# PSUM banks by turns, denser weight splits and a reordered first root in an attention and gated feed-forward kernel

## The chip, the cores and the metric

The kernel runs on one core of one Trainium2 chip. A core has a matrix engine (PE, TensorE) with its own weight loads, and VectorE (DVE), ScalarE (ACT), GpSimd (POOL) and SyncE (SP); here SP only issues DMAs. PE writes to PSUM, which has eight banks; DVE and ACT read PSUM, POOL does not. Each engine works through its own list of instructions in order, and semaphores hold it where it needs another engine's result. The metric is the time of one execution on the device in microseconds (us).

## The reference

All tensors are float32. Attention has 8 batches, 8 heads, 576 positions and heads of 64; the first four heads see the last 32 positions, the other four every fourth of the last 128. Its output, 4608 rows of 512, goes through a normalization by the root of the mean square and a gated feed-forward layer of width 1536:

```python
scores = where(mask[h], q @ k.T / sqrt(64), -1e9)        # per batch and head
attn = exp(scores - max) / (sum + 1e-9)
x = (attn @ v) -> rows of 512
xn = x / sqrt(mean(x * x) + 1e-6) * rms_g
g, val = xn @ w_gate, xn @ w_val                         # 512 -> 1536
out = (g * sigmoid(g) * val) @ w_out                     # 1536 -> 512
```

## The kernel before, in words

**Items.** The 4608 rows are worked in 16 items `u` of 288 rows, each half of one batch. An item has two kinds of work: its attention, in 14 bursts (a pair of heads `c` and a block `i` of rows), and its feed-forward, in 12 slices `j` of 128 of the 1536 columns. While item u's feed-forward runs, the attention of item u+1 is woven into it.

**Steps.** The main loop (L783 to L811) has a step `t` for every third of a slice: part 0 is the gate (L643: 128 columns of `w_gate` by the four chunks of xn, which accumulate in one PSUM bank), part 1 the value (L667, same form with `w_val`), part 2 the projection (L693) of the slice before, which adds into four banks acc0 to acc3. Item u has the steps 36u to 36u+35. Ahead of the main loop run 25 rounds `n` (L765) with the attention of item 0 alone and the first of item 1; in them `busy` (L731) puts filler matmuls on PE, whose result nobody reads, and `start` (L628) already runs gate and value of slice 0 on the unnormalized rows. Round n has the clock `now` = n; step t has now = t + 23.

**Order.** It is written out by hand. `later(dt, rank, fn)` (L110) puts work off by dt rounds or steps; `flush` (L113) issues what is due, by rank, at the start of each. So the queue of each engine is filled by step and then by rank: a normalization of scores for item 2 and later has rank -1, a product 0, the copy out of a transposition 0.2, the copy of an attention output 0.5, the tanh of a gate 0, silu 0.8, exponentials 2, weight decoding 5 and up, weight splits 6.

**A burst** goes through scores on PE (L486, or L489 from item 2 on), maximum and mask (L361, L366, DVE), exponential (L376, ACT), normalization (L384 to L391; on POOL, DVE or ACT), transposition on PE (L463) into a PSUM bank, copy to SBUF (L446 on ACT, and L448 on DVE for the low part from item 2 on), output on PE (L472, L477, L478) and copy into the rows `xraw` (L408, L411, L421). `plan` (L740) says in which round or step each of these three PE parts runs. From item 3 on, bursts come every two steps, so that their transpositions fall on all three parts in turn; those of item 1 fall on parts 0 and 1.

**The root.** When the last burst of an item is out, `square` (L423) squares each chunk of its rows, the squares are added (L433), PE sums them over the columns (L529, tile `rps`), DVE and POOL form the power -1/2 (L536, L537), DVE (and ACT, from item 1 on) spreads it into diagonal tiles (L551 and L555, or L561 for item 0), PE spreads that over the partitions (L571, tile `bps`), and DVE multiplies the rows with it (L582 for item 0, L585 later).

**Banks.** Gates always take the bank g, values the bank v, and each uses 288 of the bank's 512 columns. A transposition in the main loop writes to columns 288 to 479 of such a bank:

```python
if part == 0:   free = gate(u, j)        # the gate just written
elif part == 1: free = val(u, j)         # L805 then puts it back to this slice's gate
else:           free = v_free            # this slice's value
```

Readers of the gate's bank are tanh (ACT, L656) and silu (DVE, L661), the reader of the value's is the product (DVE, L674); a write to a bank waits for its readers. In the rounds, transpositions alternate between g and v (L772), scores between s, acc0 and acc1, outputs between o and acc2.

**Weights.** They arrive as 64-bit floats in 18 pieces of two slices; `rebase` (L151, ACT or POOL), and `shift`, `low`, `sign` or `rest`, `whole` (L164 to L183, DVE) make float32 of them during the rounds and item 0, whose matmuls use that float32 (L619). From item 1 on each weight is a sum of two rounded parts, and each gate has three matmuls (L622 to L624) for every one; `split_weight` (L227) makes the parts, high on ACT (L242), low on DVE or POOL (L243), into SBUF that earlier tiles leave free. The tuple SPLITS says at which steps: at even steps from 8 to 30, then from step 37 in four of five, until all 36 slices are done.

Of the kernel before, what the change touches and what calls it, by code (L numbers as in the profile page):

```python
# [9 lines left out]
F32 = mybir.dt.float32  # L10
# [24 lines left out]

LAG, OUT, LATER = 4, 2, 1
STEPS = (0,) * 6 + (1, 0) * 2 + (1,) * 4 + (0,) * 9 + (2, 1)
REBASES = 5, 9, 17, 20
BUSY = 7, 3
SIGNS = 4  # L40
SPLITS = 8, 31, 37


ORDER = [(0, 0, "q"), (0, 1, "q"), (0, 0, "v"), (0, 2, "q"), (0, 0, "w"), (0, 1, "v"), (0, 3, "qv"), (0, 2, "v"),
# [23 lines left out]
def attn_moe(ctx: ExitStack, tc: tile.TileContext, qk_in, v_in, w_gate, w_val, w_out, rms_g, outT):  # L68
# [41 lines left out]
    def later(dt, rank, fn):  # L110
        put_off.setdefault(now[0] + dt, []).append((rank, fn))
# [283 lines left out]
    def take(u, c, i, o):  # L395

        blocks, nq, _ = geometry(u, c)
        if (u, c) not in xraw:
            xraw[u, c] = sb.tile([P, U], F32, tag="xraw", name=f"xraw_{u}_{c}", bufs=NC)
        x = xraw[u, c]  # L400
        if c < NC // 2:
            to = x[:, QB * i:QB * i + nq]
        else:
            to = x.rearrange("p (j r) -> p r j", r=DIL)[:, i, :]
        copy = V.tensor_copy if i % 2 and u != 1 else A.copy
        if u < NNAT:
            for a in range(2):
                copy(out=to[a * D:(a + 1) * D], in_=o[a * D:(a + 1) * D, a * nq:(a + 1) * nq])  # L408
        else:
            for a in range(2):  # L410
                A.copy(out=to[a * D:(a + 1) * D], in_=o[a * D:(a + 1) * D, (2 + a) * nq:(3 + a) * nq])  # L411
        if i == len(blocks) - 1:
            later(1, 2.5, lambda: square(u, c))

    def add(u, c, i, o):
        _, nq, _ = geometry(u, c)
# [211 lines left out]
    def start(kind, c):  # L628
# [2 lines left out]
            first[kind] = ps.tile([P, 512], F32, tag={"g": "acc1", "v": "acc3"}[kind], name=f"{kind}_0_0")  # L631
        three(first[kind][:, :U], weight(kind, 0, 0), c, xraw[0, c], c == 0, c == NC - 1)

    def group(kind, u, j):

        if u + j == 0:
            return first.pop(kind)
        out = ps.tile([P, 512], F32, tag=kind, name=f"{kind}_{u}_{j}")
        for c in range(NC):
            three(out[:, :U], weight(kind, u, j), c, xs[u][c], c == 0, c == NC - 1)  # L640
        return out
# [89 lines left out]
    def busy(n):  # L731

        for _ in range(n):
            PE.matmul(busy_ps, ones, ones[:, None, :].to_broadcast([P, 4, P]), start=True, stop=True)
# [5 lines left out]
    def plan(u, base, q_at, t_at, o_at):  # L740
        for b, *ts in zip(bursts(u), q_at, t_at, o_at):
            for kind, t in zip("qto", ts):
                events.setdefault(base + t, {})[kind] = b
        events.setdefault(base + o_at[-1] + 3, {})["sum"] = u
        events.setdefault(base + o_at[-1] + (4, 7, 5)[min(u, 2)], {})["apply"] = u

    def attend(t_ps, **tags):
        e = events.pop(now[0], {})
        if any(k in e for k in "qto"):
            products(e.get("q"), e.get("t"), e.get("o"), t_ps, **tags)  # L750
        if "sum" in e:
            rms_sum(e["sum"])
        if "apply" in e:
            rms_apply(e["apply"])
# [10 lines left out]
    for n in range(ends):  # L765
        decode(STEPS[n])
        if n in REBASES:
            later(0, 8, ahead)
        flush()
        t_ps = None  # L770
        if "t" in events.get(n, {}):
            t_ps = ps.tile([P, 512], F32, tag="gv"[n % 2], name=f"t_first_{n}")[:, :2 * QB]  # L772
        attend(t_ps, s_tag=("s", "acc0", "acc1")[n % (3 if n < nb else 2)], o_tag=("o", "acc2")[n % 2])
        if n < nb + LAG + OUT:
            busy(BUSY[1])
        for kind, c in FIRST.get(n, ()):
            start(kind, c)
        if n == ends - 1:
            _, v_free = gate(0, 0), val(0, 0)
        now[0] += 1  # L780

    prev = None
    for u in range(NU):  # L783
        for j in range(NJ):
            for part in range(0 if u + j else 2, 3):
                t = 3 * (u * NJ + j) + part
                if used and (t % 5 != 1 if t >= SPLITS[2] else t % 2 == 0 and SPLITS[0] <= t < SPLITS[1]):
                    later(0, 6, lambda: split_weight(*used.pop(0), V if t < SPLITS[1] or t % 2 else G))
                if u == 0:
                    decode(1)  # L790
                opening = len(ops) <= 2
                flush()
                if opening and not late:
                    early.close()
                    late.append(ctx.enter_context(tc.tile_pool(name="late", bufs=2)))
                if part == 0:
                    free = gate(u, j)
                elif part == 1:
                    free = val(u, j)
                else:  # L800
                    if prev is not None:
                        proj(*prev)
                    prev = (u, j)
                    free = v_free
                if part == 1:  # L805
                    g_free, v_free = g_free, free
                    free = g_free
                elif part == 0:
                    g_free = free
                attend(free, s_tag="acc2" if t < 4 else "s")  # L810
                now[0] += 1  # L811
    flush()
# [69 lines left out]
```

## Time and profile before

| what | us |
|---|---|
| median of 3 runs | 1155.4 (1155.17 to 1156.75) |
| profiled execution | 1156.42 |
| its span, first to last instruction | 1154.6 |
| PE busy | 1122.5 (97%) |
| DVE busy | 790.7 (68%) |
| ACT busy | 719.3 (62%) |
| POOL busy | 618.0 (54%) |
| mean granted clock of PE | 0.999 of full |

How to read what follows: a row of a timeline is start, duration, engine, line, operation, what it writes and reads with its shape, and how many instructions are merged in it; in brackets stands the idle time of the engine just before and what ended it. Rows of the chain of waits are start, duration and what the chain ran through. A matmul's duration overlaps with the next one's, so the distance of the starts counts. A wait is put down to the semaphore that came last, which may name an instruction just beside the true one.

### The profile page before, as it was taken

To read this page: it belongs to the slowest core of one execution; us is meant where nothing else is said; L and a number is where in the kernel's file an instruction comes from. 1 tells how busy PE (TensorE), PEld (TensorE's weight loads), DVE (VectorE), ACT (ScalarE), POOL (GpSimd) and SP (SyncE) were. 2 spreads that over 40 slices of the span, in tenths; PEclk is the share of its full clock that TensorE was granted. 3 is DMA by queue.
4 is the path that set the end of the run, shared out by engine and by line. 5 is a ranking of instruction groups with operands and counts; after the bars stand their busy time and mean duration, and the time that the engine had idled before them with its cause. 6 is when DMAs were issued, how large, how long until landed. Compare 5 with 4: busy or idle time off the path is not lost.

```text
span 1154.6 us, 25970 instructions
## 1 busy us (share of the span) xinstructions
PE 1122.5 (97%) x8363; PEld 1086.7 (94%) x8363; DVE 790.7 (68%) x2900; ACT 719.3 (62%) x2602; POOL 618.0 (54%) x1074
## 2 busy tenths in 40 slices
PE   8898879999999999999999999999999999999998
PEld 6686778999999999999999999999999999999998
DVE  7889866866757586675758667585866757586421
ACT  5686576665757576575756657576765757676311
POOL 7235567655646465564646655465655646565211
PEclk9999999999999999999999999999999999999999
DMA  8556211211312122131212213131221313120000
GB/s 245 152 202 211 92 50 38 82 58 41 93 37 82 40 70 63 44 97 28 84 41 79 60 40 92 29 93 38 72 63 34 101 30 88 38 81 15 1 22 21
DMA packets 61545, 82.19 MB, mean 71 GB/s; under 512 B 7298, under 2 KB 41090, under 8 KB 61410
## 3 DMA queue, kind: packets, MB, share of 16 engines
q1 hardware_dynamic: 61410, 80.54, 23.3%
q8 instruction: 67, 1.10, 0.4%
q14 instruction: 68, 0.56, 0.2%
HBM read 71.08 MB, written 9.44 MB: 70 GB/s over the span
## 4 chain that ended last, share of the span: by engine, by line
PE 77%; DVE 15%; ACT 4%; issue 2%; POOL 1%; DMA 0%; POOLq 0%; SPq 0%; DVEq 0%; ACTq 0%
PE acc L622 8%; PE acc L623 7%; PE acc L624 7%; PE g L622 7%; PE v L622 7%; PE v L623 7%; PE v L624 7%; PE g L624 7%; PE g L623 7%; DVE qs L344 3%; PE s L489 3%; PE o L477 3%; PE g L463 2%; DVE xraw L585 2%; DVE t L366 2%
## 5 line engine op out<-in xcount | busy, mean ns | idle before, releaser
L686 POOL TENSOR_TENSOR hlo<-th,hhi 128x288 fp32r<-128x288 f32 x180 | 145.1, 806 | 193.4 <-ACT hhi L685 189.6
L624 PE MATMUL acc<-hhi,lo 128*128 128x288 f32 x720 | 212.5, 295 | 0.0
L391 POOL TENSOR_SCALAR t<-t,sum 72x72 f32<-72x72 f32 (+3 forms) x414 | 151.0, 377 | 82.0 <-DVE sum L386 72.8
L624 PE MATMUL v<-xhi,lo 128*128 128x288 f32 x612 | 180.7, 295 | 0.0
L624 PE MATMUL g<-xhi,lo 128*128 128x288 f32 x612 | 180.6, 295 | 0.0
L685 ACT CAST hhi<-th 128x288 fp32r<-128x288 f32 x180 | 78.1, 434 | 162.6 <-DVE th L674 159.3
L376 ACT ACTIVATE t<-t,sum 96x128 f32<-96x128 f32 (+3 forms) x448 | 165.7, 376 | 14.1 <-DVE sum L366 13.4
L305 POOL TENSOR_TENSOR vlo<-vt,vhi 128x128 fp32r<-128x128 f32 x196 | 94.3, 481 | 116.3 <-ACT vhi L301 99.5
L421 DVE TENSOR_TENSOR xraw<-o,xraw 64x96 f32<-64x96 f32 (+1 forms) x392 | 106.8, 272 | 60.8 <-ACT xraw L411 55.8
L656 ACT ACTIVATE th<-g 128x288 f32<-128x288 f32 x180 | 73.9, 411 | 119.1 <-PE g L624 92.3
L624 PEld LDWEIGHTS acc<-hhi,lo 128*128 128x128 f32 x720 | 135.7, 188 | 0.0
L661 DVE SCALAR_TENSOR_TENSOR th<-th,g 128x288 f32<-128x288 f32 x180 | 80.4, 447 | 68.6 <-ACT th L656 68.6
L361 DVE TENSOR_TENSOR t<-s,mask 96x256 f32<-96x256 f32 (+3 forms) x196 | 71.7, 366 | 77.8 <-PE s L489 57.2
L624 PEld LDWEIGHTS v<-xhi,lo 128*128 128x128 f32 x612 | 115.2, 188 | 0.0
L624 PEld LDWEIGHTS g<-xhi,lo 128*128 128x128 f32 x612 | 115.0, 188 | 0.0
L411 ACT COPY xraw<-o 64x96 f32<-64x96 f32 (+1 forms) x392 | 101.7, 259 | 16.3 <-PE o L478 14.0
L622 PE MATMUL g<-xhi,hi_g 128*128 128x288 f32 x357 | 110.6, 310 | 0.4 <-DVE pt L448 0.3
L622 PE MATMUL acc<-hhi,hi_o 128*128 128x288 f32 x360 | 110.9, 308 | 0.0
L335 POOL TENSOR_TENSOR ks<-qk,ks 128x288 fp32r<-128x288 f32 (+2 forms) x112 | 110.3, 999 | 0.0
L623 PE MATMUL acc<-hlo,hi_o 128*128 128x288 f32 x360 | 107.1, 298 | 0.0
L674 DVE TENSOR_TENSOR th<-th,v 128x288 f32<-128x288 f32 x180 | 81.4, 452 | 36.2 <-PE v L624 33.4
L623 PE MATMUL g<-xlo,hi_g 128*128 128x288 f32 x322 | 94.8, 294 | 0.0
(179 smaller groups left out, 3575.8 us busy)
## 6 DMA issues: line engine op xcount, KB each, us to landing
qk<-in_qk_dram SPq DMA_DIRECT2D x60, 288.0 KB, 2.8
vt<-in_v_dram SPq DMA_DIRECT2D x196, 64.0 KB, 1.9
qk<-in_qk_dram SPq DMA_DIRECT2D x30, 352.0 KB, 3.0
out_dram<-ot SPq DMA_DIRECT2D x64, 144.0 KB, 1.9
qk<-in_qk_dram SPq DMA_DIRECT2D x30, 304.0 KB, 2.8
raw<-in_w_gate_dram SPq DMA_DIRECT2D x12, 512.0 KB, 4.3
raw<-in_w_val_dram SPq DMA_DIRECT2D x12, 512.0 KB, 4.9
raw<-in_w_out_dram SPq DMA_DIRECT2D x12, 512.0 KB, 4.1
```

What stands on the lines that cost most here:

```text
L305: G.tensor_tensor(out=vl, in0=vs.pop(b), in1=vh, op=ALU.subtract)
L335: ek.tensor_tensor(out=ks[:, 1, :nkt], in0=kr, in1=ks[:, 0, :nkt], op=ALU.subtract)
L376: A.activation(out=t[:nq, a, :n], in_=t[:nq, a, :n], func=AF.Exp, scale=-1.0, bias=sm[:nq, a, 0:1], accum_out=sm[:nq, a, 1:2] if u else None)
L391: (V if u == 0 and (c, i) > (NC - 1, 0) else G).tensor_scalar(out=t[:nq, a, :n], in0=t[:nq, a, :n], scalar1=sm[:nq, a, 3:4], scalar2=1.0, ...
L411: A.copy(out=to[a * D:(a + 1) * D], in_=o[a * D:(a + 1) * D, (2 + a) * nq:(3 + a) * nq])
L421: V.tensor_tensor(out=to[rows], in0=o[rows, a * nq:(a + 1) * nq], in1=to[rows], op=ALU.add)
L622: PE.matmul(out, wh[:, cc, :], xh, start=start, stop=False)
L623: PE.matmul(out, wh[:, cc, :], xl, start=False, stop=False)
L624: PE.matmul(out, wl[:, cc, :], xh, start=False, stop=stop)
L661: V.scalar_tensor_tensor(out=t, in0=t, scalar=1.0, in1=g, op0=ALU.add, op1=ALU.mult)
L674: V.tensor_tensor(out=t, in0=t, in1=v_ps[:, :U], op=ALU.mult)
L686: G.tensor_tensor(out=lo, in0=t, in1=hi, op=ALU.subtract)
```

## The change

- Banks: gate j now takes g for even j and v for odd j, value j the other one; so gate j+1 is written to the bank of value j, and value j+1 to the bank of gate j. A transposition in part 0 goes to the gate just written (as before), in part 1 to the value just written, in part 2 to a new tile in the bank of this slice's gate.
- Splits: the first stretch begins at step 4, not 8 (even steps up to 30); from step 37 on every step has one.
- Opening: the last rebase on ACT moves from round 20 to 23; the square of item 0 gets rank 1.9 instead of 2.5; from round 17 on one filler matmul a round instead of three; in item 0 the odd bursts of the first three chunks are copied by ACT instead of DVE; the transposition of round 24 goes to acc0, the scores of rounds 21 to 24 alternate between s and acc2 instead of s and acc0.
- Item 1's sums (L529) run one step later; its root's spread (L571) stays where it was.

```diff
-REBASES = 5, 9, 17, 20
+REBASES = 5, 9, 17, 23
-SPLITS = 8, 31, 37
+SPLITS = 4, 31, 37
...
-        copy = V.tensor_copy if i % 2 and u != 1 else A.copy
+        copy = V.tensor_copy if i % 2 and u == 0 and c == NC - 1 else A.copy
...
-            later(1, 2.5, lambda: square(u, c))
+            later(1, 2.5 if u else 1.9, lambda: square(u, c))
...
+    def bank(kind, j):
+        return "gv"[(j + (kind == "v")) % 2]
...
-        out = ps.tile([P, 512], F32, tag=kind, name=f"{kind}_{u}_{j}")
+        out = ps.tile([P, 512], F32, tag=bank(kind, j), name=f"{kind}_{u}_{j}")
...
-        events.setdefault(base + o_at[-1] + 3, {})["sum"] = u
+        events.setdefault(base + o_at[-1] + (4 if u == 1 else 3), {})["sum"] = u
...
-            t_ps = ps.tile([P, 512], F32, tag="gv"[n % 2], name=f"t_first_{n}")[:, :2 * QB]
-        attend(t_ps, s_tag=("s", "acc0", "acc1")[n % (3 if n < nb else 2)], o_tag=("o", "acc2")[n % 2])
+            t_ps = ps.tile([P, 512], F32, tag="gv"[n % 2] if n < nb + LAG else "acc0", name=f"t_first_{n}")[:, :2 * QB]
+        s_tags = ("s", "acc0", "acc1") if n < nb else ("s", "acc0") if n < nb + LAG + OUT else ("s", "acc2")
+        attend(t_ps, s_tag=s_tags[n % len(s_tags)], o_tag=("o", "acc2")[n % 2])
         if n < nb + LAG + OUT:
-            busy(BUSY[1])
+            busy(BUSY[1] if n < nb + LAG - 1 else 1)
...
-                if used and (t % 5 != 1 if t >= SPLITS[2] else t % 2 == 0 and SPLITS[0] <= t < SPLITS[1]):
+                if used and (t >= SPLITS[2] or t % 2 == 0 and SPLITS[0] <= t < SPLITS[1]):
...
-                    free = v_free
-                if part == 1:
-                    g_free, v_free = g_free, free
-                    free = g_free
-                elif part == 0:
-                    g_free = free
+                    free = None
+                    if "t" in events.get(now[0], {}):
+                        free = ps.tile([P, 512], F32, tag=bank("g", j), name=f"t_{u}_{j}")[:, :2 * QB]
```

(`nb` is 14, `LAG` 4, `OUT` 2.)

More of the change, by code (lines that the diff above doesn't have):

```diff
@@ L778, in attn_moe @@
         if n == ends - 1:
-            _, v_free = gate(0, 0), val(0, 0)
+            gate(0, 0)
+            val(0, 0)
         now[0] += 1
```

## The prediction

> **What bounds the kernel now.** I first cut the span into stages and read each engine's busy time in each (start:end, length, then busy us and instructions of PE, PE weight loads, DVE, ACT, POOL; granted clock, DMA share, GB/s), then PE's waits by what ended them (last three columns: us in total, times, longest).
>
> ```profile
> 0.00:34.00 34.00, 28.80 (x162) 22.60 (x163) 25.75 (x120) 17.03 (x59) 23.92 (x58) 1.00 0.86 248
> 34.00:47.00 13.00, 10.96 (x65) 8.82 (x63) 9.31 (x34) 7.18 (x24) 4.11 (x5) 1.00 0.38 68
> 47.00:95.00 48.00, 46.38 (x235) 36.58 (x236) 40.47 (x110) 41.91 (x131) 15.17 (x11) 1.00 0.59 211
> 95.00:132.35 37.35, 30.99 (x138) 23.40 (x136) 34.46 (x54) 18.39 (x47) 19.09 (x19) 1.00 0.42 143
> 132.35:206.00 73.65, 62.81 (x464) 59.61 (x465) 50.50 (x183) 52.94 (x182) 49.64 (x75) 1.00 0.18 52
> 206.00:1154.60 948.60, 942.53 (x7306) 935.70 (x7304) 630.20 (x2404) 581.83 (x2163) 506.07 (x907) 1.00 0.19 57
> ...
> PE g L463 <- DVE sum L385: 1.8, 7, 0.3
> ```
>
> From 206 us on PE is the bound: 942.5 of 948.6 us, and of the 6.1 us left 1.8 are transpositions (L463) held back in seven places. Nothing can be won there but those 1.8 us and the end. Before 206 us three stages have slack. The opening (to 47 us) is a chain through PE, ACT, DVE and POOL. Item 0's gates and values run from 47 to 132 us: PE-bound at first (46.4 of 48), then DVE-bound (34.5 of 37.4, while PE idles 6.4). Item 1's stage, 132 to 206 us, has PE idle for 10.8 us with no engine full, so it waits on order. The change must pay in these three, and a gain there reaches the end as it is, since what follows 206 us starts when PE gets there.
>
> **The opening.** The rows below are pieces of the chain of waits (start, us), then rows of the timelines.
>
> ```profile
> 30.83 0.19 DVE xraw L408
> ...
> 31.04 0.29 DVE xraw L408
> ...
> 34.99 0.70 PE busy L734 x3
> ...
> 35.93 0.69 PE busy L734 x3
> ...
> 38.18 0.57 ACT t L376 x3
> 38.75 0.34 ACT sq L427
> ...
> 36.58 1.16 ACT L159 ACTIVATE f<-raw 128x1024 f32<-128x1024 f32 x1
> ...
> 40.18 0.59 PE L529 MATMUL rps<-inv,sq 128*96 128x2 f32 x6
> ...
> 44.36 1.04 PE L486 MATMUL s<-qk 128*96 128x128 f32 x8
> ...
> 44.67 0.81 DVE L582 TENSOR_TENSOR xn<-xraw,bps 128x288 f32<-128x288 f32 x2
> ...
> 46.92 2.21 PE L619 MATMUL g<-xn,f 128*128 128x288 f32 x8 [1.52 <-ACT pt L446]
> ```
>
> The copies: in item 0 the odd bursts 1, 4, 7 and 9 go from DVE to ACT, two copies each, 0.19 + 0.29 us a burst on the chain (first two rows: burst 7). The chain runs through three of the four, 1.4 us. ACT has the room (busy 17.0 of the first 34 us, DVE 25.8), but takes its work in order and may free a bank late, so I count 1.0.
> The fillers: three rounds lose two of three filler matmuls, two thirds of 0.70, 0.47 us each. Two of the triples stand in the chain, the third just behind it on PE, which then runs without a gap to the sums' matmuls (rps) at 40.18: 1.4 us.
> The square and the rebase: the square of the last chunk stood behind the rebase (1.16 us) and three exponential pieces on ACT and ended at 39.09; it now goes ahead of both. This gives nothing by itself, because PE reaches rps at 40.18 only through its own order; but without it the chain would hold PE once the fillers go. The rebase, three rounds later, falls into a stretch in which ACT waits for a sum, and its reader on DVE (the shift of step 2) is two rounds on.
> Together rps, the root and the normalized chunks (xn, done at 45.48) come 2.4 us earlier.
> The transposition's bank: round 24 wrote to the bank that gate group 1 needs, so the gate began at 46.92, after ACT's copy (pt), though PE was free at 45.40 and xn ready at 45.48. The transposition now goes to acc0 and the gate to a bank read long before: 1.4 us more. **Opening: 3.8 us**, at least 1.4 (the bank alone), at most 5.0 (copies in full, and a bank wait that ends with them).
>
> **Item 0's gates and values.**
>
> ```profile
> 52.13 0.38 PE L463 MATMUL g<-ident,t 96*128 96x96 f32 x2 [0.54 <-DVE sum L385]
> ...
> 108.62 0.64 PE L529 MATMUL rps<-inv,sq 128*96 128x2 f32 x6 [2.60 <-DVE sq L433]
> ...
> 112.42 0.46 DVE L551 TENSOR_TENSOR rd<-ident,rst_hi 96x288 fp32r<-96x288 f32 x1 [1.01 <-POOL rst_hi L542]
> ...
> 121.56 2.10 PE L619 MATMUL g<-xn,f 128*128 128x288 f32 x8
> ...
> 123.81 0.44 DVE L674 TENSOR_TENSOR h<-h,v 128x288 f32<-128x288 f32 x1
> ...
> 128.62 0.44 PE L489 MATMUL s<-ks,qs 128*96 128x256 f32 x2 [2.11 <-DVE sum L366]
> ...
> 62.37 0.61 ACT L242 CAST hi_g<-f 128x512 fp32r<-128x512 f32 x1
> ```
>
> The wait of 0.54 us is a part-1 transposition waiting for its gate's bank (for silu); it goes. The two splits added at steps 4 and 6 put 2 x 0.61 us on ACT and about as much on DVE, where the next product and normalization queue behind them; ACT is 87% busy in this stage. I set 0.5 us against the 0.54, with 0 to 1.2 as bounds.
> The sums of item 1 come one step later, so PE may run a gate group (2 us) in place of the 2.60 us wait. I do not count that as PE time: the stage is DVE's, and by the new banks that gate needs the product before it, which DVE finishes only around 108. What does count is on DVE: the root's POOL work, for which DVE idles 1.01 us, then has a step of DVE work beside it. So 1.0 us, with 0 to 2.6 as bounds.
> The banks add a wait here: gate j+1 needs the bank of value j, hence product j. Gate group 11 began at 121.56, its product came at 124.25: PE will stand 2.7 us. But PE's next scores wait for DVE in any case until 128.6 in this stage, and the gate's reader on DVE comes later than the delayed gate would end, so I price it at nothing; without that cover it costs up to 2.7 us. **Item 0: 1.0 us.**
>
> **Item 1's stage.**
>
> ```profile
> 145.56 0.34 PE L463 MATMUL v<-ident,t 96*96 96x96 f32 x2 [1.46 <-DVE th L674]
> 145.68 0.36 PE L489 MATMUL s<-ks,qs 128*72 128x144 f32 x2
> 145.88 0.34 PE L622 MATMUL g<-xhi,hi_o 128*128 128x288 f32 x1
> ...
> 159.56 0.29 PE L463 MATMUL g<-ident,t 72*72 72x72 f32 x2 [2.43 <-DVE sum L385]
> ...
> 162.41 0.31 PE L622 MATMUL g<-xhi,hi_g 128*128 128x288 f32 x1
> ...
> 159.60 0.43 DVE L674 TENSOR_TENSOR th<-th,v 128x288 f32<-128x288 f32 x1
> ...
> 151.46 0.97 DVE L243 TENSOR_TENSOR lo<-f,hi_o 128x512 fp32r<-128x512 f32 x1 [1.67 <-ACT hi_o L242]
> ...
> 202.38 1.11 DVE L243 TENSOR_TENSOR lo<-f,hi_g 128x512 fp32r<-128x512 f32 x1 [2.50 <-ACT hi_g L242]
> 203.41 1.11 DVE L551 TENSOR_TENSOR rd<-ident,rst_hi 96x288 fp32r<-96x288 f32 x1
> ...
> 204.66 0.51 PE L571 MATMUL bps<-rd,ones 96*128 96x288 f32 x2 [2.16 <-DVE rd L551]
> ...
> 202.50:204.66 2.16, 0.00 (x0) 0.03 (x1) 2.16 (x3) 1.21 (x5) 1.70 (x2) 1.00 0.01 4
> 206.20:209.50 3.30, 3.30 (x17) 3.30 (x16) 3.20 (x11) 0.77 (x2) 1.66 (x4) 0.50 0.60 160
> ```
>
> The 2.43 us wait is a part-1 transposition behind silu. With the value's own bank it is gone, and PE runs on through the projection; but then the gate waits for product 159.60 + 0.43 = 160.03 instead of starting at 162.41, so 2.4 us at most; DVE is behind at that point and its next product will not come earlier by as much, so I take 1.75, with 0 as the other bound. Where a part-2 transposition waited for a product (145.56), the wait does not go, it moves to the gate: only the transposition and scores in between (0.3 to 0.5 us) slip under it. Four such places, 0.2 to 0.4 each: 1.0.
> The denser splits give both ways. Steps 41, 46, 51 and 56 get a split that they did not have, and DVE stands in line for ACT's half of one (1.67 us idle, then 0.97) in the worst row, nothing in the best. I take 1.5 us lost over four, with 0 to 3.0 as bounds. In return steps 59 to 65 have none. The split at step 65 is what held up rd: DVE waited 2.50 us for ACT, ran 1.11, and only then made rd for bps. Without it rd follows its POOL input, and of the 2.16 us I count 1.6.
> Behind that wait the clock fell to 0.50 for 3.3 us (second-last and last row); at half clock 3.3 us do the work of 1.65. I count 1.0 of it: with a shorter gap the drop may go, but a new gap can cause another.
> [...] **Item 1: 1.75 + 1.0 - 1.5 + 1.6 + 1.0 = 3.85 us**; its bounds are 3.0 lost (splits alone) and 2.4 + 1.2 + 2.16 + 1.65 = 7.4 won.
>
> **The PE-bound rest.**
>
> ```profile
> 772.72 0.45 DVE L674 TENSOR_TENSOR th<-th,v 128x288 f32<-128x288 f32 x1
> ...
> 773.45 0.38 PE L622 MATMUL g<-xhi,hi_g 128*128 128x288 f32 x1
> ...
> ACT th L656 <- PE g L463: 21.5, 33, 1.1
> ```
>
> The seven part-1 waits (1.8 us in all) go: 1.6. The new wait of a gate on the product before is free so long as the product ends first. The pair shown is the tightest of the 169 after 206 us: product done at 773.17, gate 0.28 us later. I went through all of them; half leave over 1 us. A product now also has to let a part-1 transposition finish in its own bank, as tanh does in 33 places today (last row); that is two transpositions, 0.2 us of PE, less than the 0.28.
> [...]
>
> **The sum.** 3.8 + 1.0 + 3.85 + 1.6 = 10.25 us. The profiled execution took 1156.42 us (span 1154.6 and 1.8 around it), so 1146.2; it lies 1.0 above the median of the three runs, 1155.4, from which it would be 1145.2. I take **1145.7 us**, its own range 1140 to 1150.
>
> **Rivals.** (1) Only the opening pays. The first half of item 0 is PE-bound and carries it, but in item 1 waits move more than they go: products come no earlier, and the added splits eat the rest. Opening 3.8 + item 0's 1.0 = 4.8: 1151 (1150 to 1153). For it: the three waits on L674 are DVE's. Against: the 2.43 and 2.16 us waits are not. (2) Nothing: DVE is full from 95 to 132 us, and an earlier start is lost if that stretch is tied to something fixed, such as weights still on their way, while the gain of item 1 is eaten by splits: 1155. Against it: each load there is issued by the end of the decode before it, so it moves with it. (3) Slower: a gate behind a late product, all through the PE-bound rest. It decides once products end over 0.28 us later than now, in the tight units first. If a third of the 168 gates there (14 items of 12) wait 0.25 us, that costs 14 us against the 8.65 won before: 1161. For it: PE works in order and has nothing ahead of that gate. Against it: half of the pairs have over 1 us.
>
> **How the numbers follow.** The forecast 0.62, only the opening 0.21, nothing 0.09, slower 0.08. About 0.2% (2.3 us) is what a measurement here can tell from none, so the first two are faster: 0.83; same 0.09; slower 0.08. All bounds at their best (5.0 + 3.1 + 7.4 + 1.8) give 17.3 us, 1139; at their worst, without rival 3, they give 1159. At that end the range takes in rival 1 and stops short of rival 2: 1139 to 1153.5.
>
> **What would show it.** Right: gate group 1 starting near 43 us with no wait on pt; rps of item 0 near 38; bps of item 1's stage with no wait over 0.6 us and no row of half clock behind it; no part-1 wait at L463 on silu. Wrong: PE waits on L674 at the gates (L622) after 206 us, above all more than ten of them; DVE idle before L243 growing between 140 and 185 us; or an item 0 stage that ends at 132 us as before although it began 4 us earlier.

## The result and the profile after

| | before | after |
|---|---|---|
| median, us (4 runs each, by turns) | 1155.91 | 1148.38 |
| range, us | 1155.17 to 1156.75 | 1148.1 to 1149.65 |
| profiled execution, us | 1156.42 | 1148.22 |
| its span, us | 1154.6 | 1146.4 |

The ratio is 0.9937 (95% interval 0.992 to 0.9954): faster by 7.5 us, 8.2 between the two profiled executions. The forecast was 1145.7 us; its sum of gains, 10.25 us, taken from the profiled execution alone gave 1146.2. Code lines behind L634 are 5 higher than before (product L679, silu L666, tanh L661).

The stages of after, cut 4 us earlier than those of before (same columns):

```profile
0.00:34.00 34.00, 30.92 (x177) 24.12 (x178) 24.46 (x116) 20.55 (x71) 26.76 (x60) 1.00 0.95 250
34.00:43.00 9.00, 8.67 (x51) 7.01 (x50) 8.05 (x29) 5.27 (x19) 2.49 (x4) 1.00 0.50 93
43.00:91.00 48.00, 44.41 (x221) 35.13 (x220) 40.07 (x112) 40.59 (x129) 13.45 (x9) 0.96 0.58 208
91.00:128.00 37.00, 32.70 (x141) 24.52 (x140) 34.36 (x52) 20.84 (x51) 20.49 (x18) 1.00 0.40 141
128.00:202.00 74.00, 63.94 (x462) 60.89 (x462) 51.05 (x184) 50.66 (x175) 49.68 (x77) 0.98 0.19 55
202.00:1146.40 944.40, 940.18 (x7314) 936.32 (x7312) 635.40 (x2405) 576.67 (x2167) 507.90 (x908) 1.00 0.20 57
```

PE fills the opening better (30.92 of the first 34 us, before 28.80), but the clock is below full in two stages where it was full before, 0.96 and 0.98, and from 43 to 91 us PE idles 3.6 us.

PE's waits over the whole span (us, times, longest), and those from 202 us on:

```profile
PE g L619 <- DVE h L679: 3.7, 4, 1.5
PE v L622 <- DVE pt L448: 3.3, 2, 1.8
PE s L486 <- DVE sum L366: 2.8, 1, 2.8
```

```profile
PE o L477 <- ACT pt L446: 0.4, 1, 0.4
PE acc L623 <- POOL hlo L691: 0.2, 1, 0.2
```

The seven part-1 waits are gone, and no gate waits for a product behind 202 us: rival 3 did not happen. The first three rows are new or grown, and all lie before 202 us. The first is the priced gate wait of item 0, four times; the third is the scores at step 5.

**Shift of the steps.** For the rest I use one measure: the start of the first matmul of a step's group (gate, value or projection) in one trace, minus the same step's start in the trace of before. Negative is earlier.

| step | 3 | 5 | 7 | 36 | 66 | 72 | 74 | 575 |
|---|---|---|---|---|---|---|---|---|
| shift after, us | -5.33 | -6.19 | -1.46 | -2.56 | -0.55 | -4.49 | -4.23 | -8.19 |

So the opening gave 5.3 us; item 0 won 0.9 more, lost 4.7 in the next two steps and won 1.1 back up to step 36; item 1 lost 2.0 up to step 66, then won 3.7 at its root; the PE-bound rest gave 4.0. The place of the loss, in PE's timeline and in the stages around it:

```profile
51.85 0.58 PE L486 MATMUL s<-qk 128*72 128x104 f32 x4 [2.83 <-DVE sum L366]
52.27 3.81 PE L619 MATMUL g<-xn,f 128*128 128x288 f32 x8
```

```profile
52.00:54.00 2.00, 2.00 (x8) 1.56 (x8) 2.00 (x7) 1.84 (x4) 0.00 (x0) 0.58 0.96 389
54.00:56.00 2.00, 2.00 (x6) 1.30 (x6) 1.04 (x2) 1.64 (x7) 1.69 (x1) 0.57 0.09 20
```

PE stood 2.83 us, and then ran a gate at half clock, 3.81 us instead of 2.11. What it stood for, in the timeline of all engines:

```profile
49.70 0.60 ACT L242 CAST hi_g<-f 128x512 fp32r<-128x512 f32 x1
...
50.33 0.69 DVE L243 TENSOR_TENSOR lo<-f,hi_g 128x512 fp32r<-128x512 f32 x1 [0.45 <-ACT hi_g L242]
50.94 0.45 DVE L679 TENSOR_TENSOR h<-h,v 128x288 f32<-128x288 f32 x1
51.30 0.28 DVE L366 CUSTOM_DVE_ANT_0 t<-s,mask 96x128 f32<-96x128 f32 x1
51.42 0.32 ACT L446 COPY pt<-v 128x192 f32<-128x192 f32 x1 [1.12 <-DVE h L679]
```

This is the split of step 4. DVE waits for ACT's half, makes its own, and only then comes to the product and to the masks (L366) for which PE's scores stand: 0.45 + 0.69 = 1.14 us.

### The profile page after: what moved, and what is told of

It reads as the page before. It is cut to its first block, busy times and chain, and to the rows that moved or that the text cites. A ratio compares the mean times of both kernels' runs of the same rounds, so it can differ in the third digit from the quotient of the medians.

```text
span 1146.4 us, 25956 instructions
## 1 busy us (share of the span) xinstructions
PE 1120.8 (98%) x8357; PEld 1088.0 (95%) x8357; DVE 793.4 (69%) x2893; ACT 714.6 (62%) x2610; POOL 620.8 (54%) x1073
## 4 chain that ended last, share of the span: by engine, by line
PE 85%; DVE 6%; ACT 4%; issue 2%; DMA 1%; POOL 1%; POOLq 0%; SPq 0%; DVEq 0%; ACTq 0%
PE acc L622 8%; PE g L622 8%; PE v L622 8%; PE acc L623 8%; PE g L624 8%; PE g L623 8%; PE acc L624 8%; PE v L623 8%; PE v L624 8%; PE s L489 3%; PE o L477 3%; PE o L478 1%; PE busy L739 1%; ACT t L376 1%; DVE lo L243 1%
## 5 line engine op out<-in xcount | busy, mean ns | idle before, releaser
L391 POOL TENSOR_SCALAR t<-t,sum 72x72 f32<-72x72 f32 (+3 forms) x414 | 154.0, 384 | 71.9 <-DVE sum L386 65.2
L661 ACT ACTIVATE th<-g 128x288 f32<-128x288 f32 x180 | 73.9, 410 | 106.6 <-PE g L624 87.7
L666 DVE SCALAR_TENSOR_TENSOR th<-th,g 128x288 f32<-128x288 f32 x180 | 80.4, 447 | 69.4 <-ACT th L661 69.4
L679 DVE TENSOR_TENSOR th<-th,v 128x288 f32<-128x288 f32 x180 | 81.5, 453 | 38.1 <-PE v L624 30.0
```

What stands on the lines that cost most here:

```text
L391: (V if u == 0 and (c, i) > (NC - 1, 0) else G).tensor_scalar(out=t[:nq, a, :n], in0=t[:nq, a, :n], scalar1=sm[:nq, a, 3:4], scalar2=1.0, ...
L666: V.scalar_tensor_tensor(out=t, in0=t, scalar=1.0, in1=g, op0=ALU.add, op1=ALU.mult)
L679: V.tensor_tensor(out=t, in0=t, in1=v_ps[:, :U], op=ALU.mult)
```

## The experiments

Each edit is on the changed kernel, but for the one that starts from the kernel before. The table has shifts against before. Two cautions.

The first is a late start. The first scores start at 5.4 to 5.5 us in every trace, but filler matmuls take longer until PE's clock first rises to full: in before one takes 0.63 us at 7.07 us and 0.40 at 8.54, with the rise at 8.25. Below are three of them, first in before, then in e1:

```profile
6.07 1.63 PE L734 MATMUL busy<-ones 128*128 128x512 f32 x3
```

```profile
5.85 0.94 PE L739 MATMUL busy<-ones 128*128 128x512 f32 x3
```

In the profiled executions of before, after, e4 and e11 the clock rose at 7.95 to 8.27 us, in the others at 5.33 to 7.00. So the first transposition of a probability tile started at 11.0 to 11.2 us in those four, and at 10.2 to 10.6 in the others. Among the runs with the changed opening this moves step 3 by up to 0.8 us, and I compare like with like or by differences between steps.

The second is the clock later on. The last column has the starts of the stretches at half clock (granted clock 0.50), without one at the very end. Each lasts 3.41 us, in which PE does at most 1.7 us less work (half of 3.41, by the granted clock). Before has one, at 206.2.

| run | edit | ratio (95%) or single time | 3 | 7 | 36 | 66 | 74 | 575 | half clock from, us |
|---|---|---|---|---|---|---|---|---|---|
| after | | 0.9937 (0.992 to 0.9954) | -5.33 | -1.46 | -2.56 | -0.55 | -4.23 | -8.19 | 52.3, 147.9 |
| e1 | first split at step 8 | 0.9911 (0.9896 to 0.9926) | -5.95 | -4.91 | -5.46 | -2.80 | -6.49 | -9.94 | 145.6 |
| e2 | four of five from step 37 | 0.9922 (0.9905 to 0.9939) | -5.96 | -2.42 | -3.88 | -3.44 | -6.45 | -9.33 | 50.6 |
| e8 | first at 8, none at 41, 46, 51 | 0.9915 (0.9901 to 0.993) | -5.91 | -4.87 | -5.02 | -4.26 | -6.93 | -10.27 | none |
| e4 | old banks | 0.9971 (0.996 to 0.9982) | -5.16 | -1.85 | -2.61 | -0.05 | -3.55 | -3.35 | 49.2, 158.5 |
| e7 | turned banks alone, on before | 0.9971 (0.9959 to 0.9982) | -2.45 | -1.40 | +0.58 | +1.26 | +1.11 | -1.96 | 108.3 (two in a row), 173.1, 207.3 |
| e9 | part 1 in the gate's bank | 0.9958 (0.9942 to 0.9975) | -5.94 | -3.77 | -4.45 | -2.61 | -6.09 | -5.66 | 146.0 |
| e5 | old opening | 0.9967 (0.9954 to 0.998) | -2.45 | -0.26 | +0.11 | +2.79 | -0.89 | -3.85 | none |
| e6 | old step of the sums | 0.995 (0.9935 to 0.9966) | -5.74 | -1.93 | -2.00 | +0.06 | -3.63 | -7.32 | 51.4 |
| e10 | three fillers | 1150.5 (one) | -4.85 | -1.00 | -2.45 | -0.43 | -4.13 | -5.95 | 53.1, 148.7 |
| e11 | odd copies on DVE | 1151.44 (one) | -2.95 | -0.77 | -0.48 | +1.48 | -2.20 | -4.99 | none |
| e12 | old square and rebase | 1147.22 (one) | -5.89 | -3.69 | -4.29 | -1.50 | -5.45 | -9.19 | 145.7 |
| e13 | e8, and part 1 in the gate's bank until step 72 | 0.9927 (0.9906 to 0.9948) | -5.93 | -4.30 | -4.55 | -3.21 | -5.72 | -8.60 | 156.4 |

### The splits

```diff
-SPLITS = 4, 31, 37
+SPLITS = 8, 31, 37
```

> The changed kernel with the first stretch of splits from step 8 again (SPLITS 8, 31, 37), all else as changed. Theory: the split of step 4 stands DVE in line behind ACT, holds PE's scores of step 5 for 2.8 us and lets the clock fall for 3.4 us behind it; without it gate group 2 (step 6) starts 2.5 us earlier, at about 49.8 us, the clock stays full there, steps 7 to 20 run 4 us earlier than in the changed kernel, and since the DVE-bound stretch moves along, the time falls by 3 us to about 1145.3. Rival: DVE is full from 43 to 52 us without the split too (decode and product), the wait shrinks by the split's 0.7 us alone, and the DVE-bound stretch from 91 us on takes up what is left: within 1 us of the changed kernel, 1148.

Measured: 1146.38 us beside 1156.69. In PE's timeline the scores of step 5 still wait, 1.16 us less, and no half clock follows there:

```profile
50.09 0.58 PE L486 MATMUL s<-qk 128*72 128x104 f32 x4 [1.67 <-DVE sum L366]
50.50 2.12 PE L619 MATMUL g<-xn,f 128*128 128x288 f32 x8
```

From step 3 to 7, 1.0 us of the lead is lost here and 3.9 in after. The early split costs 1.16 us of wait, and where the clock falls behind it, 1.7 more. Some wait is left without it: DVE is not earlier by as much as PE. The time lies between the theory's 1145.3 us and the rival's 1148; of the 3.45 us that e1 is ahead of after at step 7, 1.75 are left at the end, and 0.6 of both is the late start of after.

```diff
-if used and (t >= SPLITS[2] or t % 2 == 0 and ...):
+if used and (t % 5 != 1 if t >= SPLITS[2] else t % 2 == 0 and ...):
```

> The changed kernel with splits in four of five steps from step 37 on, as before; all else as changed (splits still from step 4). Theory: the added split of step 41 makes the 1.78 us wait of a value on its bank's low copy near 147 us and the half clock behind it (about 1.7 us), so both go and item 1's first half is 2 to 3 us faster; but splits now end at step 62 instead of 58 and one may stand before the root's spread again. Net -2 us, 1146.4. Rival: the denser splits are what removed the 2.16 us wait of bps and the half clock behind it; with the old density both come back and the time is 2 us longer, 1150.5.

Measured: 1147.26 us beside 1156.69, 0.9 from the theory. From step 36 to 66 this run loses 0.4 us, after 2.0; yet it wins 3.0 of after's 3.7 at the root. So the denser splits cost 1.6 us in item 1. After's trace has a stretch of half clock there and this one has none, but e6 and e11, with the denser splits and no half clock there, lose 2.1 and 2.0 us too. The root's spread hardly needs the denser splits: with two more early splits the last one comes at step 63, not 65.

```diff
-SPLITS = 4, 31, 37
+SPLITS = 8, 31, 37
...
-if used and (t >= SPLITS[2] or t % 2 == 0 and ...):
+if used and (t not in (41, 46, 51) if t >= SPLITS[2] else t % 2 == 0 and ...):
```

> The changed kernel with the first stretch of splits from step 8 and none at steps 41, 46 and 51 (the last one falls on step 63), all else as changed. Theory: it keeps the 3.4 us that the split of step 4 cost and the 2 us plus half clock that the split of step 41 cost, and the root's spread of step 65 stays free of a split, so bps has no wait: step 74 at 8.5 us ahead of before, against 6.7 with the first alone; 2 us faster than that one, 1144.5 on its scale. Rival: a half clock or a split's queue turns up elsewhere as soon as these go, and it is within 0.7 us of the kernel with splits from step 8 alone, 1146.4.

Measured: at step 66 it is 1.5 us ahead of e1, at step 74 0.4, at the end 0.3, and the ratio is the same, as the rival said. What the splits at steps 41, 46 and 51 cost is mostly repaid at the root, where e1 has its last split at step 60 and this run at step 63.

### The banks

```diff
-out = ps.tile([P, 512], F32, tag=bank(kind, j), ...)
+out = ps.tile([P, 512], F32, tag=kind, ...)
...
-free = None
-if "t" in events.get(now[0], {}):
-    free = ps.tile([P, 512], F32, tag=bank("g", j), ...)[:, :2 * QB]
+free = v_free          # and part 1 back to the gate's columns, as before
```

> The changed kernel with the banks of before (gates in g, values in v, part 1 transposed into the gate's bank, part 2 into the value's), all else as changed. Theory: behind 206 us the 0.36 us at the last projection of each item come back, 4.7 us in all less about 1 elsewhere, so it loses 3.7 there; before 206 us, gates no longer stand behind products (3.7 us of waits of L619 on the product in the changed kernel go) and the copy of a part-1 transposition no longer behind a product, so the scores' wait at step 5 falls below 1.7 us; at step 66 it is 0 to 3 us ahead of the changed kernel. End: about 1149.5 on this chip's scale, 0 to 3 us longer than the changed kernel. Rival: the banks help before 206 us as well (silu's 2.43 us at step 49 comes back): 5 us longer than the changed kernel.

Measured: 1153.01 us beside 1156.22. At step 36 this run and after lie within 0.1 us, at step 74 it is 0.7 behind, and from there to the end it wins nothing (-3.55 to -3.35), where after wins 4.0. Its waits from 202 us on, beside after's (above), have the part-1 row of before again:

```profile
PE g L463 <- DVE sum L385: 1.9, 7, 0.3
```

So the whole gain of the PE-bound rest is the banks', and hardly any of the gain before it. The opening keeps its gain at step 3 too: either turned banks or the move of round 24's transposition to acc0 frees gate group 1, and the two are no sum.

```diff
-    ...tag=kind, name=f"{kind}_{u}_{j}")          # on the kernel before
+    ...tag=bank(kind, j), name=f"{kind}_{u}_{j}")
...                                                # and the new places of transpositions
```

> The kernel before with the banks by turns alone (gates and values in g and v by turns, transpositions in the bank just written or the past gate's), all else as before. Theory: the part of the gain that lies behind 206 us, 3.7 to 3.9 us in steps of 0.3 to 0.5 us at the last projection of each item, is the banks' alone, and the 1.4 us of gate group 1 too; item 1's stage gains at most 1: 1155.9 - 5 = 1151. Rival: the steps behind 206 us come from where the items start against the DMA and the splits, not from the banks: within 2 us of before, 1154.

Measured: 1153.31 us beside 1156.69, with 3.1 us won behind step 74 (after: 4.0). Up to step 74 it loses 1.1 us, with the old wait of bps at 2.2 us. This trace has four stretches of half clock where before's has one, so that the turned banks by themselves lose there is not shown. The gate's own wait at step 3 is the distance from rps to gate group 1: 46.92 - 40.18 = 6.74 us before, 5.06 here (39.41 and 44.47) and in after. So the bank is worth 1.7 us there.

```diff
-free = val(u, j)
+val(u, j)
+free = None
+if "t" in events.get(now[0], {}):
+    free = ps.tile([P, 512], F32, tag=bank("g", j), ...)[:, :2 * QB]
```

> The changed kernel with the banks by turns, but part 1 transposes into a new tile in the gate's bank instead of the value just written (as before the change, so it waits for silu); all else as changed. Theory: the 0.36 us won at the last projection of each item behind 206 us are the part-1 transposition's alone, so they go, 4.7 us, and the copies of these transpositions no longer wait for products (L446 on the product: 101 us in 70 waits falls by about half, since part 2 copies share no bank with a product). Time 3.5 to 5 us longer than the changed kernel: 1152.5. Rival: the turns themselves win it, by giving a gate a bank read a step earlier; then it is within 1 us of the changed kernel.

Measured: 1151.44 us beside 1156.22, with nothing won behind step 74 (-6.09 to -5.66), and with the part-1 waits back (1.8 us, seven times, now as tile t). Turning the banks alone gives nothing there; placing part 1's transposition behind the value gives it all. Below is that place in item 11 (steps 430 and 431), first before, then after:

```profile
888.39 0.29 PE L624 MATMUL v<-spare,lo 128*128 128x288 f32 x1
888.96 0.36 PE L463 MATMUL g<-ident,t 96*128 96x96 f32 x2 [0.29 <-DVE sum L385]
889.10 0.38 PE L622 MATMUL acc<-hhi,hi_g 128*128 128x288 f32 x1
```

```profile
881.69 0.30 PE L624 MATMUL v<-spare,lo 128*128 128x288 f32 x1
881.83 0.33 PE L463 MATMUL v<-ident,t 96*128 96x96 f32 x2
881.94 0.38 PE L622 MATMUL acc<-hhi,hi_g 128*128 128x288 f32 x1
```

From the last value matmul to the projection it took 0.71 us, now 0.25: 0.46 won where the wait is shown as 0.29. In items 2 to 13 the projection at that step comes 0.31 to 0.48 us earlier, 4.7 us in these twelve, of which some 0.8 is given back at other steps. The ten other runs with the new place of part 1 behind step 74 win the same 4.6 to 4.8 us at these projections, but give back more and keep 1.8 to 3.7; so the 4.0 us of after is the most that any of them kept.

### The opening

```diff
-REBASES = 5, 9, 17, 23      # and copies, square, round 24, scores' banks, fillers
+REBASES = 5, 9, 17, 20      # all as before; banks, splits and sums stay changed
```

> The changed kernel with the whole opening of before (rebase in round 20, square at rank 2.5, three fillers in every round, odd copies on DVE, round 24's transposition in the bank g or v, scores between s and acc0), all else as changed. In this form gate group 1 takes bank v, so round 24's transposition in g doesn't hold it. Theory: the opening is worth 3.9 us at gate group 1 (5.3 less the 1.4 of the bank, which stays), but the wait at step 5 shrinks when PE comes later, so step 7 is only about 0.5 us later than in the changed kernel, and the end 0.5 to 1 us: 1149. Rival: the opening's gain reaches the end as a whole: 1152.3.

Measured: 1152.88 us beside 1156.69, as the rival said. The wait at step 5 is 2.82 us, as long as in after, although PE comes later; the theory had it shrink. The ratio is 0.9967 against 0.9937, so the opening is worth 3.5 us of the 7.5 at the end (0.0030 of 1156), while the turned banks alone already give what this run has at step 3. The next three take the rest apart; I read them at rps, which came 3.65 us earlier in after than before (40.18 to 36.53).

```diff
-busy(BUSY[1] if n < nb + LAG - 1 else 1)
+busy(BUSY[1])
```

> The changed kernel with three filler matmuls again in every round of the opening, nothing else. In the changed kernel's trace gate group 1 (step 3) starts at 41.59 us and rps of item 0 at 36.53. Theory A (the prediction's step: two of the triples stood in the chain and the third just behind it on PE, 3 x 0.47 us): both move back by 1.2 to 1.6 us, rps to about 37.9 and gate group 1 to about 43.0. Rival B (the chain runs beside the fillers, and the copies and the order of square and rebase gave the 2.9 us): both move by less than 0.4 us.

```diff
-copy = V.tensor_copy if i % 2 and u == 0 and c == NC - 1 else A.copy
+copy = V.tensor_copy if i % 2 and u != 1 else A.copy
```

> The changed kernel with the odd bursts of item 0 copied by DVE again, nothing else. Theory A (the prediction's step: three of the four bursts stand in the chain of waits, of 1.4 us I counted 1.0): rps and gate group 1 start 0.8 to 1.4 us later, near 37.5 and 42.6. Rival B (the chain of the opening is set by ACT's exponentials and PE's rounds, so DVE has the time for the copies): less than 0.3 us. Since the three opening edits together gave 2.9 us at gate group 1, a sum of this run and the one with three fillers above 2.9 would mean that both hold the same piece of the chain.

```diff
-REBASES = 5, 9, 17, 23
+REBASES = 5, 9, 17, 20
...
-later(1, 2.5 if u else 1.9, lambda: square(u, c))
+later(1, 2.5, lambda: square(u, c))
```

> The changed kernel with the last rebase on ACT back in round 20 and the square of item 0 behind the exponentials again, nothing else. Theory A (the prediction's step: worth nothing by itself before, but with the fillers gone the chain through ACT would hold PE): the copies and fillers are gone here, so the wait shows at rps: a wait of PE on DVE's sum of squares (L433), and rps 0.7 to 1.5 us later than 36.53. Rival B (ACT has slack at that place once PE runs earlier): rps within 0.3 us of 36.53.

Measured, the row of rps: after and the copies run (both with the late start), then three fillers, old square and rebase, and e13 as the changed opening with the early start:

```profile
36.53 0.59 PE L529 MATMUL rps<-inv,sq 128*96 128x2 f32 x6
```

```profile
38.91 0.59 PE L529 MATMUL rps<-inv,sq 128*96 128x2 f32 x6
```

```profile
37.01 0.59 PE L529 MATMUL rps<-inv,sq 128*96 128x2 f32 x6
```

```profile
35.90 0.67 PE L529 MATMUL rps<-inv,sq 128*96 128x2 f32 x6
```

```profile
35.93 0.59 PE L529 MATMUL rps<-inv,sq 128*96 128x2 f32 x6
```

Like with like: the copies 38.91 - 36.53 = 2.4 us, the fillers 37.01 - 35.93 = 1.1, square and rebase 0.0. That makes 3.5 of the 3.65 us, so they add up; the 2.9 us in the expectation was too small, since e5 had the early start. Each of the three is one execution, but the five traces with the changed opening and an early start (e1, e2, e8, e9, e13) have rps within 0.05 us of each other. The copies are worth more than either theory said, the fillers a little less than the first, square and rebase what the rival said. Against plain after, the fillers would have shown only 0.5 us: the late start would have hidden half of the term. In the copies run's waits of PE in the opening stand, as in those of before, two rows; in after only 0.2 us of the first:

```profile
PE t_first L463 <- POOL t L391: 2.1, 3, 1.0
...
PE o L472 <- DVE xraw L408: 0.5, 2, 0.3
```

2.1 + 0.5 - 0.2 = 2.4. The copies were on the chain in a second way: DVE's copies stood ahead of its sums of the next burst, POOL's normalization (L391) waited for those (4.5 us up to 36 us in the copies run, 1.7 in after), and PE's transposition for POOL.

### Sums, and a version put together

```diff
-events.setdefault(base + o_at[-1] + (4 if u == 1 else 3), {})["sum"] = u
+events.setdefault(base + o_at[-1] + 3, {})["sum"] = u
```

> The changed kernel with item 1's sums at their old step (26), all else as changed. Theory of the prediction: POOL's root then has no DVE work beside it, DVE idles about 1 us before the spread again and PE waits at the sums, so steps 27 to 36 are 1.0 us later, 1149.5. Rival: with the banks by turns gate 9 waits for its product anyway, the sums' place decides nothing, and the time is that of the changed kernel within 0.5 us.

Measured: ratio 0.995 against 0.9937, 1.5 us, with intervals that overlap; by the shifts, 0.6 us at step 36 and 0.9 at the end, with 0.4 more for this run's earlier start. The theory and the rival lie too close to be told apart by it.

```diff
+if t < 72:               # on e8: part 1 as in e9, but in items 0 and 1 only
+    free = None
+    if "t" in events.get(now[0], {}):
+        free = ps.tile([P, 512], F32, tag=bank("g", j), ...)[:, :2 * QB]
```

> The changed kernel with the first split at step 8, no splits at steps 41, 46 and 51, and, in items 0 and 1 only, part-1 transpositions into a new tile in the gate's bank instead of the value's columns (from item 2 on as in the changed kernel). Theory A (behind the value, ACT's copy waits for DVE's product where DVE is late, which costs 1.9 us up to step 74, while from item 2 on the value's bank gives 0.36 us an item, and the early split costs 3.4 us at step 7, of which the end keeps 2 to 3): gate groups 7.5 to 9 us earlier than before at step 74 and 11 to 13 us at the end, 1143.5 to 1145.5 us if the kernel before takes 1156.2. Rival B (DVE and the order of the splits set items 0 and 1, whichever bank is used, once the splits are right): no more than without the other bank, a shift of 7 us at step 74 and 10.3 at the end, and a ratio within 0.0015 of 0.9915.

Measured: 1147.61 us beside 1156.44, a ratio near that of e8, as the rival said, and 1.2 us behind e8 at step 74. From e9's shift at step 74 (-6.09 against -4.23) I had read that a part-1 transposition behind the value costs 1.9 us in items 0 and 1. That reading falls. 0.6 us of it was the late start of after's profiled execution, and most of the rest can be the half clock at 52 us, which e9 did not have. Which bank is better there stays open: e13 is 0.5 us behind e8 at step 36 and 1.0 at step 66, but in between it has a stretch of half clock at 156.4 us, and e8 has none. PE's longest stand at steps 4 and 5, in e13 and in e8:

```profile
47.83 0.38 PE L463 MATMUL t<-ident,t 96*128 96x96 f32 x2 [2.27 <-DVE h L666]
```

```profile
50.13 0.58 PE L486 MATMUL s<-qk 128*72 128x104 f32 x4 [1.68 <-DVE sum L366]
```

In e13 the transposition waits for silu, in e8 the scores for the masks.

The best versions are e1 and e8, 1146.4 and 1146.7 us; their ratios lie 0.0026 and 0.0022 below that of the changed kernel, but the intervals overlap, so that they beat it is likely and not shown.

## Why the prediction was right, and where it was not

Direction and range were right (1148.4 in 1139 to 1153.5, and in the likeliest case's own 1140 to 1150). The sum was 2 us too good, and that it was so near is partly luck: its four terms were each off by 1.5 to 3.8 us, and the errors offset each other.

| term | forecast | measured by the shifts |
|---|---|---|
| opening | 3.8 | 5.3 |
| item 0 | 1.0 | -2.8 |
| item 1 | 3.85 | 1.7 |
| PE-bound rest | 1.6 | 4.0 |
| sum | 10.25 | 8.2 |

**Opening.** Right in the mechanisms of the fillers and of the bank, wrong in the size of the copies and in one argument. Fillers 1.4 forecast, 1.1 measured; square and rebase nothing by themselves, measured 0.0, but the enabling I gave them did not show: with the fillers gone, PE still did not wait for the old order. Bank 1.4, measured 1.7. The copies I priced at 1.0 by their own durations on the chain; they were worth 2.4, above my bound of 1.4. The waits they caused on POOL and PE were in the profile, 2.1 and 0.5 us, and I had not put them to the copies' account.

**Item 0: the step that failed.** "I set 0.5 us against the 0.54, with 0 to 1.2 as bounds" for the splits at steps 4 and 6. The added wait, 1.16 us, was within the bounds, but two things were missing. One is the half clock behind the longer wait (1.7 us). The other is that DVE would be late at step 5 even without the early split, once gate group 1 need not wait for its bank: the scores wait 1.67 us in e1 and in e7, whose opening is the old one (e4 has 2.3 us at the part-1 transposition instead). The edits of the opening do not cause it, because PE's gate and DVE's work both follow the normalized chunks xn. The masks that the scores wait for, in before (xn ended at 45.48), and xn and these masks in e1:

```profile
53.78 0.28 DVE L366 CUSTOM_DVE_ANT_0 t<-s,mask 96x128 f32<-96x128 f32 x1
```

```profile
40.40 0.80 DVE L582 TENSOR_TENSOR xn<-xraw,bps 128x288 f32<-128x288 f32 x2
...
49.54 0.28 DVE L366 CUSTOM_DVE_ANT_0 t<-s,mask 96x128 f32<-96x128 f32 x1
```

The masks start 8.30 us behind the end of xn in before, 8.34 in e1 and 8.33 in e7. But gate group 1 starts 1.45 us behind xn in before, and 0.23 us ahead of its end in e7 and e1. PE won these 1.7 us alone, and without the early split 1.05 of them are lost again by step 7 (e1, e7, e8). I had asked what DVE's lateness does from 95 us on, and not what it does at 47 us, where the stage's row said PE-bound. That row was true of the kernel before because PE had stood for the bank just ahead of it. The later sums, forecast 1.0, gave 0.6 to 1.5. The gates behind products stood 3.7 us in four places and cost nothing, as priced: at step 36 old banks and new are 0.05 us apart, both with the late start and one half clock.

**Item 1.** The root's part was right and a little small: bps no longer waits, the half clock behind it is gone, 3.7 us against 1.6 + 1.0. The denser splits cost 1.6 us by e2, forecast 1.5. What failed is the gain of 1.75 and 1.0 from the turned banks: with old banks the run loses 2.6 us from step 36 to 66, with new ones 2.0, each with one half clock there, so some 0.5 of 2.75 came. The waits moved on to the next thing that DVE makes, as rival 1 had it for this stage; after's longest there is a value behind DVE's copy of a low part (1.78 us, at 147.04), with half clock behind it once more.

**PE-bound rest.** Right in kind, 1.6 against 4.0 in size. I added up the idle time that the profile shows for seven waits. The cost of a wait is the distance of the starts: 0.46 us where 0.29 is shown, because the row of the last matmul covers part of the gap (in after it lasts 0.30 us and the next start comes 0.14 behind its own); and twelve items paid, not only the seven with a wait long enough to be listed. That after kept 4.0 us of it is in part luck: the other runs kept 1.8 to 3.7. The tightest pair, 0.28 us, held: no gate waits on a product there.

**The signs.** Gate group 1 at 41.59 us, rps at 36.53, no part-1 wait and no wait of bps over 0.3 us came as the signs of being right. Of the signs of being wrong one came in part: item 0's stage began 5.3 us earlier and ended only 2.6 us earlier. DVE's idle time before L243 between 140 and 185 us went from 4.0 to 4.4 us.

## What to carry to other kernels

A gain that one engine gets alone is lost at the next engine that is late, here 1.05 of the bank's 1.7 us, while one that both get goes through. So ask of each term which engines it moves, and do not take "PE-bound" from a trace in which PE was held up just ahead. Take a removed wait by the distance of starts and not by its idle time, and take a moved copy with the waits it causes on other engines. Before comparing two traces' shifts, check that they agree at a point ahead of the edit: here 0.6 us of start and a half clock that comes and goes led one reading astray and leave another open.

## What the runs showed of the hardware

**The same wait had half clock behind it in four traces and not in three.** Seven traces have the same wait of 2.81 to 2.83 us at step 5 (after, e2, e5, e6, e10, e11, e12). In after, e2, e6 and e10 the clock fell to 0.50 for a stretch around its end, in e5, e11 and e12 not. The old square and rebase run:

```profile
51.30 0.58 PE L486 MATMUL s<-qk 128*72 128x104 f32 x4 [2.83 <-DVE sum L366]
51.71 2.13 PE L619 MATMUL g<-xn,f 128*128 128x288 f32 x8
```

Its gate takes 2.13 us where after's takes 3.81. What differs is where the wait lies on a grid. In all 14 traces each stretch at half clock starts a whole number of 3.41 us behind the clock's first rise, and lasts 3.41 us (once 6.83): 58 times 3.413 us behind the rise at 8.25 in before, 13 and 41 times behind the one at 7.95 in after. Below are two windows of that grid around the wait, first in after, then in the old square and rebase run (the first two numbers behind the window are its length and PE's busy time, the third last is the granted clock):

```profile
48.91:52.32 3.41, 0.58 (x6) 0.47 (x6) 2.93 (x10) 1.86 (x7) 0.00 (x0) 1.00 0.34 117
52.32:55.73 3.41, 3.41 (x10) 2.38 (x9) 2.45 (x7) 3.32 (x10) 1.69 (x1) 0.50 0.47 193
```

```profile
46.68:50.09 3.41, 1.79 (x9) 1.17 (x7) 2.78 (x6) 3.02 (x12) 1.29 (x1) 1.00 0.05 18
50.09:53.50 3.41, 2.20 (x12) 1.84 (x13) 3.38 (x14) 2.20 (x6) 0.00 (x0) 1.00 0.87 310
```

In after the whole wait falls into one window, PE idles 2.83 of its 3.41 us, and the next window has half clock. In the other run an edge cuts the wait into 1.62 and 1.21 us, and the clock stays. Over the 14 traces the window ahead of a stretch at half clock has at least 1.78 us of PE idle in 15 of 16 cases (1.57 in the other), and the windows behind the first rise that none follows have at most 1.75, but for two in e11 (1.83 and 1.87). In before the one has 1.86 us, and in after the two have 2.83 and 1.78, where the longest idle time that none follows is 1.70. So in these traces about half a window of idle time stood ahead of a half clock, in after the wait of 2.83 us and that of 1.78 us at 147.04. PE's timeline of after:

```profile
147.04 0.40 PE L622 MATMUL v<-xhi,hi_o 128*128 128x288 f32 x1 [1.78 <-DVE pt L448]
...
147.67 0.29 PE L623 MATMUL v<-xlo,hi_o 128*128 128x288 f32 x1
147.80 0.36 PE L624 MATMUL v<-xhi,lo 128*128 128x288 f32 x1
147.96 0.44 PE L622 MATMUL v<-xhi,hi_o 128*128 128x288 f32 x1
148.20 0.44 PE L623 MATMUL v<-xlo,hi_o 128*128 128x288 f32 x1
...
151.25 0.33 PE L624 MATMUL acc<-hhi,lo 128*128 128x288 f32 x1
151.41 0.29 PE L622 MATMUL acc<-hhi,hi_o 128*128 128x288 f32 x1
```

The starts go from 0.13 to 0.24 us apart near 147.9 and back near 151.3. So the low stretch, on record from 147.89 to 151.31 us, comes 0.9 us behind the end of the wait, at the edge of the window that held it.

**Two readers of one PSUM bank stood in line in after.** There ACT's copy of a part-1 transposition waits for DVE's product, 101.2 us in 70 waits from item 1 on and 3.4 in three in item 0, though the two read different columns; the rows of ACT's waits:

```profile
ACT pt L446 <- DVE th L679: 101.2, 70, 2.5
...
ACT pt L446 <- DVE h L679: 3.4, 3, 1.1
```

Neither before nor e9 has such a row. Behind 202 us PE stands 0.4 us for it in all; ACT is busy for 577 of the 944 us there. What makes the copy wait is not shown beyond e9, where the tile lies elsewhere and the rows are gone.
